# A windowed-attention and gated-MLP kernel: the first entry's values loaded behind its queries and keys, three of them by ScalarE's queue

## The chip, the cores and the metric

The kernel runs on one core of one Trainium2 chip. The metric is the device time of one launch in microseconds (us). TensorE, the matrix engine, is called PE; the others are VectorE (DVE), ScalarE (ACT), GpSimd (POOL) and SyncE (SP), which here only issues DMAs.

## The reference, cut to what matters

Attention over 8 batch entries, 8 heads, 576 positions and 64 dimensions per head, with a causal window; then the attention's output, 4,608 tokens of 512, goes through an MLP with a gate.

```python
scores = scale * np.matmul(q, k.transpose(0, 1, 3, 2))
mask_plain = (rel >= 0) & (rel < 32)                               # heads 0 to 3
mask_dil = (rel >= 0) & (rel < 128) & (rel % 4 == 0)               # heads 4 to 7
attn = softmax(np.where(masks, scores, -1e9))
x = np.matmul(attn, v)          # then (B*S, H*D)
h = x @ w_in                    # 512 x 2048
g = h * (1.0 / (1.0 + np.exp(-1.702 * h)))
out = g @ w_out                 # 2048 x 512
```

## The kernel before, in words

The MLP's products are made of three matmuls each: weights and inputs are split into a high part that PE's fast type can hold and a low part that is the rest, and high x high, low x high and high x low are summed. So every weight tile has to be decoded before its first use. `decode` (line 363) does it for one tile of 128 x 512: a DMA (`fetch`, line 392), two activations on ScalarE (lines 402 and 403), a third that may go to VectorE (line 396 or 398), a shift on VectorE (line 406), an addition on VectorE or GpSimd, a copy that rounds to the high part (line 346), and a subtraction that leaves the low part (line 353). The tiles are taken in the order of lines 360 and 361: the first two of the up-projection (n = 0 and 1), the first of the down-projection (n = 2), the third of the up-projection (n = 3), and so on.

Attention works on pairs of heads; one batch entry is four pairs, so pairs 0 to 3 are the first entry. For these `first_attention` (line 683) loads queries and keys with one DMA (`load_qk`, line 435), the values with another (`load_v`, line 448), makes the scores (line 478 puts the mask into the PSUM place `sp`, line 490 adds the products to it), and then the softmax: the maximum (line 510), the subtraction (in the helper of line 353), the exponentials on ScalarE (line 514), the sum (line 526), the reciprocal (line 518), the scaling by it (line 529). There is one `sp` place, so a pair's scores wait until the subtraction of the pair before has read it. `first_transposed` (line 691) turns the weights round and `first_multiplied` (line 697) multiplies them by the values (line 576) into the four PSUM banks `first_x`; `drain_x` (line 613) copies these into `xs`, again as a high and a low part, and the next pair's product waits for that. The products of PE's matrix with `xs` (line 863, tile `hp_m`) begin the MLP's first group of tokens.

Four loads of the first entry's values are the subject here. `load_v` puts those of pair 0 into a place of their own, `v`, and those of pairs 1 to 3 into parts of `arena` that later hold other things. Line 454 tells the planner of each load: a cost of 390 (KB) on the DMA resource, an urgency (lower goes first) and the earliest time at which it may be issued (0, 4, 11 and 14 us).

The order of all instructions on every engine is made by a planner before the launch (class `Plan`). Each step is added with its possible engines and their costs, an urgency, what it reads and writes, a slack (a gap that it must keep, for a step without predecessors the earliest time), and the count of PE instructions in it. `placed` (line 111) goes through simulated time: at each turn it takes the engine that can start something first, and of the steps that can start by then the one of lowest urgency. For a DMA the simulated data come over a bus (line 203). Where PE would be idle in the first 60 us of the plan it gets filler matmuls: small ones (line 1262, up to 25 us) and full ones (line 1258, tile `idle`), whose number is counted from the idle time expected. `ordered` (line 104) plans four times, from the second time on with latest starting times worked out from the plan before, which rule from 130 us on.

`fetched` (line 134) is the planner's model of the loading of PE's instructions: these come in blocks whose edges are at instruction 193 + 256 j; the block behind one edge is asked for when PE passes the edge before, and is there some time later: 4.2 us if that was before 6 us, 6.1 us before 18 us, 4.2 us after.

```python
                part = cost * (edge - n) / count
                at = max(when + part, blocks[j])
                blocks.append(at + (4.2 if at < 6.0 else 6.1 if at < 18.0 else 4.2))
```

All DMAs of the kernel before are issued by SP (`load = nc.sync.dma_start`, line 229), in the planner's order, one after the other, on one queue.

Of the kernel before, what the change touches and what calls it, by code (L numbers as in the profile page):

```python
# [15 lines left out]
B, H, S, D = 8, 8, 576, 64  # L16
DM, DF = 512, 2048
P = 128
NC = DM // P
# [14 lines left out]
QT = 5  # L34
# [8 lines left out]
PE, ACT, DVE, POOL, DMA = range(5)  # L43
# [4 lines left out]
class Plan:  # L48
# [9 lines left out]
    def add(self, costs, urgency, work, reads=(), writes=(), slack=0.0, count=0):  # L58

        i, after = len(self.ops), set()
        for k in reads:
            after.add(self.writer.get(k))
        for k in writes:  # L70
            after.add(self.writer.get(k))
            after.update(self.readers.get(k, ()))
        for k in writes:
            self.writer[k], self.readers[k] = i, []
        for k in reads:
            if k not in writes:
                self.readers.setdefault(k, []).append(i)
        self.ops.append((costs, (urgency, i), work, after - {None, i}, slack, count))
# [32 lines left out]
    def placed(self, warm_until, soon, late=None):  # L111
# [12 lines left out]
        issued, blocks = [0], [0.0]  # L124

        def start(i, e):
            held = port[0] if e == POOL or (e == DVE and ops[i][0][e] < 0) else 0.0
            if e == DMA and ops[i][1][0] >= 2000.0 and ops[i][0][e] > 100:
                held = bus[0] - 3.0
            if e == DMA and late is not None and SINCE < ready[i][e] < late[i] - CALM and late[i] < 9.0e3:  # L130
                held = max(held, ready[i][e] + 1.2)
            return max(free[e], ready[i][e], held)

        def fetched(count, when, cost):

            n = issued[0]
            issued[0] += count
            for j in range(len(blocks) - 1, 1 << 30):
                edge = 193 + 256 * j
                if edge >= n + count or edge > 1500:  # L140
                    return when + cost
                part = cost * (edge - n) / count
                at = max(when + part, blocks[j])
                blocks.append(at + (4.2 if at < 6.0 else 6.1 if at < 18.0 else 4.2))
                when, cost, n, count = at, cost - part, edge, count - (edge - n)

        open_ = [set() for _ in free]
# [5 lines left out]
        while any(open_):  # L153
# [6 lines left out]
            when, e = min((min(start(i, e) for i in mine[e]), e) for e in range(5) if mine[e])  # L160
# [22 lines left out]
            if e == PE and when < warm_until:  # L183

                at, size = max(free[e], 1.0), 0.26 if when > 8.0 else 0.44
                if when < SHORT and blocks[-1] < when - 0.3:

                    small = min((193 + 256 * (len(blocks) - 1) - issued[0]) // 4 + 1, int((when - at - 0.1) / 0.045))
                    order.extend([(None, e)] * small)
                    at = fetched(4 * small, at, small * 0.045)  # L190
                idle = max(0, int((when - max(at, 1.5) - 0.5) / size))
                fetched(2 * idle, at, idle * size)
                order.extend([(-1, e)] * idle)
            order.append((i, e))
            starts[i] = when
            if e == PE:
                cost = fetched(ops[i][5], when, cost) - when
# [19 lines left out]
def tile_windowed_attention_then_gated_mlp(  # L217
# [9 lines left out]
    nc = tc.nc  # L227
    V, A, G, T = nc.vector, nc.scalar, nc.gpsimd, nc.tensor
    load = nc.sync.dma_start
# [7 lines left out]
    add = plan.add  # L237
# [4 lines left out]
    def temp(shape, dt, tag, name):  # L242
        return tmp.tile(shape, dt, tag=tag, name=name)
# [175 lines left out]
    def lots(k):  # L419

        if 0 < k < NC:
            return f"first qk{k}", f"first v{k}"
        return "qk0", "v0"
# [15 lines left out]
    def load_v(k):  # L439
        u, place = pairs[k], lots(k)[1]  # L440

        def work(e):
            if k < NC:
                n = (QT if dilated(k) else QT + 1) * 2 * D
                flat = (None, late, main_x, left_x)[k][:, 2 * S:2 * S + n] if k else temp([P, n], F32, "v", f"v_{k}")
                u["v"] = flat.rearrange("p (s a d) -> p s a d", a=2, d=D)

                load(flat, first_v[k][:, 2 * D * (QT + 1) - n:])
                return
            flat = temp([P, 2 * NB * D], F32, "v", f"v_{k}")  # L450
            u["v"] = flat.rearrange("p (a s d) -> p a s d", a=2, s=NB)
            load(flat, vp[k - NC])

        add({DMA: 390 if k < NC else 328}, (-6.7, -6.7, -3.8, -1.6)[k] if k < NC else 1.6 * k - 0.3, work, waits(k),
            (place, place + "l"), (0.0, 4.0, 11.0, 14.0)[k] if k < NC else 0.0)

    def waits(k):

        return ["xh3.0"] if NC <= k < FIRST * NC else []

    def dilated(k):
        return k % NC >= NC // 2
# [220 lines left out]
    def first_attention(k):  # L683


        load_qk(k)
        load_v(k)
        add({PE: 1.5 if k else 2.3}, k - 1.0e5, lambda e: scores(k), (lots(k)[0],), ("sp", f"scores{k}"), count=180)
        softmax(k, k)
# [15 lines left out]
    def attention(k, urgency):  # L705
# [8 lines left out]
        if k == NC:  # L714
            load_qk(k)
            alone(k)
        load_v(k)
        if n and n > k + 1:
            if k == FIRST * NC:
# [481 lines left out]
    for i in range(4):  # L1201
# [6 lines left out]
    blocks = [Block("p", (3, 4), (dests[3], dests[4]), early_units, few=True),  # L1208
              Block("q", (5, 6), (dests[5], dests[6]), late_units),
              Block("r", (B, 7), (dests[B], dests[7]), late_units)]  # L1210
# [102 lines left out]
```

## Time and profile before

| | us |
|---|---|
| median of three timed runs | 823.56 |
| lowest and highest of them | 823.24, 824.2 |
| the profiled execution's own time | 822.45 |
| its span, from the first to the last instruction | 820.7 |
| TensorE busy in the span | 809.3 |
| VectorE, ScalarE, GpSimd busy | 669.0, 518.0, 328.4 |

A row of the timeline has the start in us from the span's start, the duration in us, the engine, the line of the kernel, the operation, what it writes and reads, and the number of like instructions that the row merges; in brackets stands the idle time of that engine before it and what ended it. PE rows are matmuls, PEld rows their weight loads, SPq rows issues of DMAs by SP. A row of the windows has the stretch, its length, then the busy time (and number of instructions) of PE, PEld, DVE, ACT and POOL, the granted clock of PE as a share, the busy share of the DMA engines and GB/s. In the list of DMA queues a row has the queue and its kind, then packets, MB and share of 16 engines' time.

### The profile page before, as it was taken

To read this page: it belongs to the slowest core of one execution; us is meant where nothing else is said; L and a number is where in the kernel's file an instruction comes from. 1 tells how busy PE (TensorE), PEld (TensorE's weight loads), DVE (VectorE), ACT (ScalarE), POOL (GpSimd) and SP (SyncE) were. 2 spreads that over 40 slices of the span, in tenths; PEclk is the share of its full clock that TensorE was granted. 3 is DMA by queue.
4 is the path that set the end of the run, shared out by engine and by line. 5 is a ranking of instruction groups with operands and counts; after the bars stand their busy time and mean duration, and the time that the engine had idled before them with its cause. 6 is when DMAs were issued, how large, how long until landed. Compare 5 with 4: busy or idle time off the path is not lost.

```text
span 820.7 us, 18890 instructions
## 1 busy us (share of the span) xinstructions
PE 809.3 (99%) x7279; PEld 653.4 (80%) x7279; DVE 669.0 (82%) x1081; ACT 518.0 (63%) x988; POOL 328.4 (40%) x294
## 2 busy tenths in 40 slices
PE   7999999999999999999999999999999999999997
PEld 4677878888887888778888888888888888888886
DVE  6898988888888876899889899996679885867575
ACT  7898986767577766786866654545456534544340
POOL 3442325455556553244345445531215332112251
PEclk9999999999999999999999999999999999999999
DMA  9577658899758657797788777775565658674545
GB/s 354 186 249 212 175 161 296 287 318 303 241 176 271 223 180 243 252 307 234 235 236 264 253 254 249 234 256 183 179 207 189 198 189 275 201 226 157 180 153 181
DMA packets 109610, 188.13 MB, mean 229 GB/s; under 512 B 26448, under 2 KB 55376, under 8 KB 109520
## 3 DMA queue, kind: packets, MB, share of 16 engines
q1 hardware_dynamic: 109376, 186.78, 70.2%
q8 instruction: 58, 0.95, 0.5%
q14 instruction: 32, 0.26, 0.1%
q10 hardware_dynamic: 144, 0.13, 0.0%
HBM read 140.64 MB, written 45.09 MB: 226 GB/s over the span
## 4 chain that ended last, share of the span: by engine, by line
PE 97%; DMA 1%; DVE 1%; issue 0%; ACT 0%; SPq 0%; DVEq 0%
PE hp_m L863 16%; PE up_p L1006 10%; PE up_r L1006 9%; PE up_q L1006 9%; PE acc_m L800 5%; PE second_p_Q L1121 5%; PE second_q_Q L1121 5%; PE acc_m L804 5%; PE acc_m L801 5%; PE second_r_Q L1121 5%; PE sp L490 4%; PE second_q_Z L1121 3%; PE second_r_Z L1121 3%; PE second_R L1121 3%; PE second_p_Z L1121 3%; PE av L608 2%
## 5 line engine op out<-in xcount | busy, mean ns | idle before, releaser
L353 POOL TENSOR_TENSOR arena<-arena 128x256 f32<-128x256 f32 (+3 forms) x94 | 100.7, 1083 | 97.8 <-DVE wi_last_units L353 21.6
L863 PE MATMUL hp_m<-xs,wi_kept 128*128 128x512 f32 x504 | 127.7, 396 | 1.2 <-DVE arena L872 0.9
L863 PEld LDWEIGHTS hp_m<-xs,wi_kept 128*128 128x128 f32 x504 | 92.9, 188 | 22.8 <-DVE arena L872 1.9
L353 POOL TENSOR_TENSOR wo_kept<-arena,wo_kept 128x512 fp32r<-128x512 f32 x41 | 56.9, 1395 | 131.5 <-ACT wo_kept L346 84.9
L346 ACT ACTIVATE wo_kept<-arena 128x512 fp32r<-128x512 f32 x111 | 69.2, 630 | 40.7 <-PE second_r_Q L1121 10.9
L1006 PE MATMUL up_r<-wi_kept,xs 128*128 128x512 f32 x336 | 85.3, 389 | 0.0
L1006 PE MATMUL up_p<-wi_kept,xs 128*128 128x512 f32 x336 | 84.2, 394 | 0.2 <-DVE arena L353 0.2
L1006 PE MATMUL up_q<-wi_kept,xs 128*128 128x512 f32 x336 | 83.4, 389 | 0.0
L1006 PEld LDWEIGHTS up_p<-wi_kept,xs 128*128 128x128 f32 x336 | 62.1, 188 | 14.7 <-DVE arena L353 0.9
L1006 PEld LDWEIGHTS up_q<-wi_kept,xs 128*128 128x128 f32 x336 | 63.0, 188 | 13.3 <-DVE arena L1028 0.3
L1006 PEld LDWEIGHTS up_r<-wi_kept,xs 128*128 128x128 f32 x336 | 63.1, 188 | 13.1
L353 DVE TENSOR_TENSOR wo_kept<-arena,wo_kept 128x512 fp32r<-128x512 f32 x80 | 61.1, 775 | 5.1 <-ACT wo_kept L346 4.7
L346 ACT ACTIVATE bt<-ct 32x256 f32<-32x256 f32 (+1 forms) x130 | 56.6, 435 | 11.7 <-DVE ct L534 6.0
L353 POOL TENSOR_TENSOR pr<-pr,sm 128x320 f32<-128x320 f32 x52 | 43.7, 856 | 48.5 <-DVE sm L518 43.5
L800 PE MATMUL acc_m<-gh,wo_kept 128*128 128x512 f32 x156 | 61.5, 394 | 0.0
L353 POOL TENSOR_TENSOR wo_kept<-wi_last_units,wo_kept 128x512 fp32r<-128x512 f32 x22 | 29.9, 1361 | 78.3 <-ACT wo_kept L346 72.3
L353 DVE TENSOR_TENSOR arena<-arena 128x512 f32<-128x512 f32 (+1 forms) x75 | 59.1, 797 | 2.7 <-ACT arena L346 1.8
L801 PE MATMUL acc_m<-gh,wo_kept 128*128 128x512 f32 x156 | 60.8, 390 | 0.0
L1027 ACT ACTIVATE arena<-arena 128x512 f32<-128x512 f32 x60 | 37.4, 628 | 33.4 <-DVE arena L353 27.2
L1028 DVE SCALAR_TENSOR_TENSOR arena<-arena 128x512 f32<-128x512 f32 x60 | 49.8, 837 | 1.7 <-ACT arena L1027 1.3
L346 ACT ACTIVATE gh<-arena 128x512 fp32r<-128x512 f32 x57 | 36.0, 631 | 17.5 <-DVE arena L872 5.8
L353 DVE TENSOR_TENSOR gl<-arena,gh 128x512 fp32r<-128x512 f32 x53 | 41.3, 779 | 6.5 <-ACT gh L346 3.2
(267 smaller groups left out, 1824.7 us busy)
## 6 DMA issues: line engine op xcount, KB each, us to landing
xs<-sums SPq DMA_DIRECT2D x168, 256.0 KB, 3.3
out_weights<-sums_o SPq DMA_DIRECT2D x63, 512.0 KB, 3.5
qk<-qk_dram SPq DMA_DIRECT2D x29, 576.0 KB, 4.4
xs<-sums_o SPq DMA_DIRECT2D x21, 512.0 KB, 3.8
v<-vp_dram SPq DMA_DIRECT2D x28, 320.0 KB, 4.1
sums_o<-arena SPq DMA_DIRECT2D x32, 256.0 KB, 3.2
sums<-arena SPq DMA_DIRECT2D x32, 256.0 KB, 2.9
arena<-wi_dram SPq DMA_DIRECT2D x15, 512.0 KB, 4.7
```

What stands on the lines that cost most here:

```text
L346: A.activation(dst, src, AF.Copy, scale=scale)
L353: (V if e == DVE else G).tensor_tensor(out=dst, in0=a, in1=b, op=op)
L490: T.matmul(dst[:, w:w + n], u["qk"][rows, at:at + 32], u["qk"][rows, S + first:S + first + n], start=not masked(k), stop=True, tile_positi ...
L608: T.matmul(u["x"][i][rows, at:at + last - first], u["v"][keys, a, m], bt[keys, m, a, first:last], start=(bank_, a) not in begun, stop=True ...
L800: T.matmul(self.acc[j], w[:, 0, cols], high, start=f == 0, stop=False)
L801: T.matmul(self.acc[j], w[:, 1, cols], high, start=False, stop=False)
L804: T.matmul(self.acc[j], w[:, 0, P * j:P * j + P], low, start=False, stop=f == NF - 1)
L863: T.matmul(hps[f], wi(f)[:, st, cols], mv[:, c], start=c == 0 and k == 0, stop=c == NC - 1 and k == 2)
L1006: T.matmul(self.banks[place], xs[:, slot, at:at + P], wi_kept[:, 2 * a + c, mv], start=fresh and c == 0 and k == 0, stop=c == 1 and k == 2 ...
L1027: add({ACT: 0.60}, -10.0, lambda e: A.activation(unit(tmp), src(), AF.Tanh, scale=0.851), need, own(tmp))
L1028: add({DVE: -0.70 if need[0][0] == "A" else 0.70}, -10.0, lambda e: V.scalar_tensor_tensor(out=unit(dst), in0=unit(tmp), scalar=1.0, in1=s ...
L1121: T.matmul(self.second[key], w[:, st, cols], mv, start=fresh and y == 0 and k == 0, stop=y == 1 and k == 2, skip_group_check=True)
```

## The change

Three things change in the code.

In `load_v`, the values of pair 0 get the urgency -2.4 instead of -6.7. So SP issues them behind the queries and keys of pairs 1 and 2 (-5.7, -4.7) and the weight tiles n = 1, 2 and 3 (-5.7, -4.6, -2.5), and just ahead of the queries and keys of pair 3 (-2.3).

The values of pairs 1 to 3 become a step of ScalarE, with a cost of 0.06 us in the plan, the urgency -50 (ahead of all else that can start) and the earliest times 16, 18 and 20 us; their DMAs are issued by `nc.scalar.dma_start`, so in ScalarE's order of instructions and on its queue. In the plan they no longer take time on the bus.

In `fetched`, the time of 6.1 us holds for edges passed before 12 us, not 18 us.

```diff
-                blocks.append(at + (4.2 if at < 6.0 else 6.1 if at < 18.0 else 4.2))
+                blocks.append(at + (4.2 if at < 6.0 else 6.1 if at < 12.0 else 4.2))
...
-                load(flat, first_v[k][:, 2 * D * (QT + 1) - n:])
+                (nc.scalar.dma_start if e == ACT else load)(flat, first_v[k][:, 2 * D * (QT + 1) - n:])
...
-        add({DMA: 390 if k < NC else 328}, (-6.7, -6.7, -3.8, -1.6)[k] if k < NC else 1.6 * k - 0.3, work, waits(k),
-            (place, place + "l"), (0.0, 4.0, 11.0, 14.0)[k] if k < NC else 0.0)
+        add({ACT: 0.06} if 0 < k < NC else {DMA: 390 if k < NC else 328}, (-2.4, -50.0, -50.0, -50.0)[k] if k < NC else 1.6 * k - 0.3,
+            work, waits(k), (place, place + "l"), (0.0, 16.0, 18.0, 20.0)[k] if k < NC else 0.0)
```

Since the plan is made from all steps at once, the order on every engine can come out differently, also far behind the opening.

## The prediction

> **What bounds the kernel now.** I read the page first, then the windows by stage, the timeline of the first 40 us and the waits.
>
> ```profile
> span 820.7 us, 18890 instructions
> PE 809.3 (99%) x7279; PEld 653.4 (80%) x7279; DVE 669.0 (82%) x1081; ACT 518.0 (63%) x988; POOL 328.4 (40%) x294
> PE 97%; DMA 1%; DVE 1%; issue 0%; ACT 0%; SPq 0%; DVEq 0%
> ...
> 0.00:40.00 40.00, 34.59 (x896) 22.77 (x897) 29.43 (x65) 33.44 (x52) 17.29 (x25) 0.96 0.72 266
> 40.00:130.00 90.00, 89.05 (x1020) 70.63 (x1019) 80.91 (x142) 79.19 (x139) 30.09 (x27) 1.00 0.67 205
> 130.00:300.00 170.00, 169.91 (x2174) 138.40 (x2174) 142.43 (x248) 122.10 (x267) 94.81 (x102) 1.00 0.78 258
> ```
>
> TensorE is the bound. The first two columns of a window are its length and PE's busy time: from 40 us on PE loses 0.95 us in 90 and then 0.09 in 170. Only in the first 40 us is there something to win: 5.41 us idle, and filler matmuls (line 1258) that count as busy. The change can act there alone, through the instant from which PE is fed without a break; every microsecond by which that instant moves moves the end by as much.
>
> The opening stage, row by row:
>
> ```profile
> 1.71 0.44 SPq L448 DMA_DIRECT2D v<-first_v_dram  x1
> 2.19 0.43 SPq L435 DMA_DIRECT2D arena<-qk_dram  x1
> 5.96 0.38 SPq L448 DMA_DIRECT2D arena<-first_v_dram  x1
> 7.22 1.34 ACT L396 ACTIVATE arena<-arena 128x512 f16<-128x512 f32 x1
> 8.71 0.74 ACT L514 ACTIVATE pr<-pr 128x640 f32<-128x640 f32 x1 [0.15 <-DVE pr L353]
> 8.74 0.71 PE L478 MATMUL sp<-plain,ident 128*128 128x320 bf16 x2 [0.65 <-DVE pr L353]
> 9.38 1.34 PEld L490 LDWEIGHTS sp<-arena 64*32 64x32 f32 x84 [0.52 <-DMA arena<-qk_dram]
> 10.58 0.67 ACT L402 ACTIVATE arena<-arena 128x512 f32<-128x512 f32 x1 [0.61 <-DMA arena<-wi_dram]
> 10.76 2.74 PE L1258 MATMUL idle<-ident 128*128 128x512 bf16 x6
> 11.73 0.82 DVE L353 TENSOR_TENSOR pr<-sp,mx 128x640 f32<-128x640 f32 x1
> 13.29 0.74 PE L478 MATMUL sp<-arena,ident 128*128 128x320 bf16 x2
> 15.03 2.33 PE L1258 MATMUL idle<-ident 128*128 128x512 bf16 x10
> 17.56 0.86 PE L490 MATMUL sp<-arena 64*32 64x64 f32 x65
> 20.25 0.37 PE L490 MATMUL sp<-arena 64*32 64x64 f32 x19 [1.83 <-issue]
> 20.55 1.49 PE L576 MATMUL first_x<-ct,v 32*64 32x32 f32 x92
> 21.96 2.63 PE L1258 MATMUL idle<-ident 128*128 128x512 bf16 x6
> 22.90 0.76 DVE L353 TENSOR_TENSOR xs<-first_x,xs 128x432 fp32r<-128x432 f32 x2
> 24.53 1.16 PE L576 MATMUL first_x<-ct,arena 32*64 32x32 f32 x92
> ```
>
> The scores of pairs 0 to 3 (line 490) follow each other through one PSUM place, each waiting for the softmax of the one before; then come the products with the values (line 576), each waiting for the drain of the one before. Pair 0's values are read first at 20.55, pair 1's at 24.53. Between them stand a hole of 1.83 us in the middle of pair 3's scores (20.25), and six fillers that took 2.63 us although the drain they cover ends at about 22.90 + 0.76 = 23.66: some 0.85 us too long.
>
> The hole is "issue": no semaphore explains it. It is the loading of PE's instructions:
>
> ```profile
> 0.00:14.38 14.38, 11.02 (x354) 6.67 (x355) 8.74 (x26) 10.06 (x15) 4.12 (x12) 1.00 0.87 332
> 0.00:20.24 20.24, 15.06 (x479) 9.08 (x479) 13.20 (x34) 15.59 (x22) 7.63 (x17) 1.00 0.91 354
> 0.00:24.60 24.60, 19.41 (x604) 11.53 (x607) 16.96 (x41) 18.88 (x30) 9.40 (x18) 0.93 0.90 345
> q8 instruction: 7, 0.11, 1.0%
> ```
>
> The PE and PEld counts give 709 instructions up to 14.38, 958 up to 20.24 and 1,211 up to 24.60, and the kernel's model (line 139) puts block edges at 705, 961 and 1,217. The seven packets of that queue up to 45 us make 16 KB each. So a block asked for at 14.38, when an edge was crossed, was there at 20.25: 5.87 us. The one asked for at 20.25 was needed at 24.60, where no such hole shows: at most 4.35 us. The Trainium skill (Runtime: NRT & Kernel Launch, Instruction fetch mechanics) has blocks of 256 instructions and calls their fetch mostly hidden: the size agrees, the 1.83 us does not.
>
> **The change, part by part.** One: pair 0's values go from third to eighth place in SP's queue. They are needed at 20.55 and five transfers later they land still far ahead of it: nothing lost. What stood behind them comes earlier:
>
> ```profile
> 5.00:10.00 5.00, 4.35 (x171) 2.73 (x175) 3.11 (x6) 4.07 (x6) 0.00 (x1) 1.00 0.99 378
> 15.00:20.00 5.00, 3.42 (x86) 1.79 (x77) 3.84 (x9) 4.67 (x7) 3.27 (x4) 1.00 1.02 408
> v<-first_v_dram SPq DMA_DIRECT2D x1, 384.0 KB, 6.2
> ```
>
> 384 KB at 378 GB/s are 1.04 us. Pair 1's queries then land near 8.3, and its wait of 0.52 us goes; the masks of the same scores start at 8.74 behind pair 0's subtraction and last 0.71 anyway, so I count 0.3. The second weight tile lands near 9.55 instead of 10.58.
>
> Two: that earlier landing changes the planner's order. With its own costs (line 203: 360 KB per us after 2 us, and 0.2 us of latency; they set an order, no time here is taken from them) the second weight tile is ready for ScalarE at 8.39 and pair 0's exponentials at 8.51. So its first activation (line 402) is now put ahead of the exponentials (line 514), where it stood behind them. In rows:
>
> ```profile
> 9.48 0.83 DVE L526 TENSOR_REDUCE sm<-pr 128x10 f32<-128x650 f32 x1 [0.20 <-ACT pr L514]
> 10.87 0.82 DVE L510 TENSOR_REDUCE mx<-sp 128x10 f32<-128x640 f32 x1 [0.56 <-PE sp L490]
> 11.61 0.20 DVE L518 RECIPROCAL sm<-sm 128x10 f32<-128x10 f32 x1
> 11.98 1.97 SPq L448 DMA_DIRECT2D arena<-first_v_dram  x2
> 12.47 0.43 DVE L406 TENSOR_SCALAR arena<-arena 128x512 uint32<-128x512 uint32 x1
> 18.65 0.67 ACT L402 ACTIVATE arena<-cell 128x512 f32<-128x512 f32 x1 [0.34 <-DMA cell<-wo_dram]
> 31.46 0.68 DVE L353 TENSOR_TENSOR wi_kept<-arena,wi_kept 128x512 fp32r<-128x512 f32 x1
> ```
>
> On the chip ScalarE is free at 7.22 + 1.34 = 8.56 and must wait for the landing near 9.55; with 0.67 for that activation the exponentials start near 10.25 instead of 8.71. VectorE then works in a row from 10.25: the second tile's shift 0.43, the first tile's low part 0.68, pair 0's sum 0.83, pair 1's maximum 0.82, the reciprocal 0.20, pair 1's subtraction 0.82. That ends near 14.05 instead of 11.73 + 0.82 = 12.55. Pair 2's scores waited behind six fillers to 13.29; they now start near 14.15: 0.85 later.
>
> Three: pairs 1 to 3's values leave SP's queue for ScalarE's, not before 16, 18 and 20 us of the plan. They are read at 24.53 and later. SP's issue of such a load lasted 0.38 (5.96); on ScalarE, 93% busy in 15:20 (4.67 of 5), three cost between nothing, if the activation before is still running, and 3 x 0.44 = 1.32, if the queue stands. No row shows one on ScalarE. The nearest row, SP's 0.38, is of an engine with no other work; on ScalarE the activation issued just before still runs for up to 1.34 (7.22), so I take 0.1 on the path. Behind a standing issue would queue the exponentials of pair 2 and the drain copies, and for these wait VectorE and PE. The Trainium skill (DMA: Bandwidth & Descriptors, Issuing engines are not separate DMA queues) says that loads of either engine share the same 16 DMA engines, so only issuing time is saved; no run here shows a second queue yet. In SP's queue the next weights move up, for which ScalarE waited 0.34 (18.65); with PE in the hole at that time, I count it at nothing.
>
> Four: the block model expects 4.2 us instead of 6.1 for edges crossed at 12 to 18 us. That only alters the count of fillers and the order, but the real fetch decides. Its edge is crossed some 0.85 us later, near 15.2. The fetch time lies between 4.35 and 5.87. For the upper end speaks that the DMA engines stay full (1.02, 408 GB/s); for the lower that the two loads issued from 11.98 on no longer stand in the queue when it is asked for. Neither row is nearer; I take 5.0. The block is there near 20.2; what is left of pair 3's scores then takes 0.5, and pair 0's product starts near 20.7 (20.55 before): +0.15. The hole shrinks from 1.83 to some 0.4 us, so the six fillers behind the product fall between 6 x 0.23 (the pitch at 15.03) and 6 x 0.44 (at 21.96), say 2.0 instead of 2.63: pair 1's product near 24.2, -0.3 against 24.53. With 0.1 for ScalarE's issues the feeding of PE starts 0.2 us earlier.
>
> From 40 us on the same matmuls follow. The whole order is planned anew, so holes can come or go: the largest one there is 0.95 (the 40:130 row), and I allow that much either way.
>
> **The sum.** The profiled execution took 822.45 (span 820.7): less 0.2 it is 822.25. The three timed runs lie 1.11 higher in the median (823.56), so 823.4. What a measurement here can tell from no change is about 0.2%, 1.65 us: from 821.9 to 825.2.
>
> **The rivals.** *Faster: the hole closes.* If the fetch takes 4.35 or less and the exponentials do not fall behind, nothing holds pair 3's scores: 1.83 go, PE keeps its clock and the fillers' 0.85 go too: 2.7 in all, 820.9. For it: the hole is the largest single loss, and the softmax chain alone had pair 3 begun by 17.56. Against it: DMA stays full, and part two delays the chain by itself. The rule quoted above from the Trainium skill (Runtime: NRT & Kernel Launch, Instruction fetch mechanics), a fetch mostly hidden, would make it so. Chance 0.22.
>
> *Slower: ScalarE's order.* The exponentials wait for a transfer they do not need. If the 1.55 us by which they are late (10.25 against 8.71) pass through all four pairs and the block, asked for later, takes its 5.87 again, the hole no longer swallows the delay; the three issues add up to 1.32, say 0.5: 2.0 in all, 825.6. It decides if pair 3's scores end after 22.1 instead of 20.62. For it: ScalarE works strictly in order and has no slack in 15:20. Against: the fillers and the hole give 0.7 and 1.83 of cover. Chance 0.17.
>
> *Nothing arrives at PE.* The values were never waited for, and if the block lands at 20.25 as before, all else is cover: 823.6. Chance 0.06; the forecast has 0.55.
>
> **How the numbers follow.** The forecast's own range is 822.2 to 824.6: 0.8 either way for the fetch time (4.35 to 5.87), the rest for ScalarE's issues. The range of 8 in 10 reaches into both rivals, to 821.1 and 825.3. Faster by over 0.2% has the first rival and a little of the forecast's edge, 0.25; slower the second and as little, 0.19; the rest, 0.56, is no difference.
>
> **What would show it.** Right: line 402 before the first line 514 on ScalarE, that exponential near 10.2; pair 2's masks near 14.2; an "issue" hole of under 1 us in pair 3's scores; pair 0's product at 20.4 to 21.0 and pair 1's at 23.9 to 24.6; ScalarE's three issues between 16 and 21 us with no wait of PE on a load of values; PE full from 40 us on but for about 1 us. Wrong: no issue hole and pair 1's product before 23 (the first rival), pair 3's scores ending past 22 (the second), a product that waits for its values, or new idle time of PE over 1 us after 40 us, which would show that the order of the rest decided.

## The result, and the profile after

| | before | after |
|---|---|---|
| median of the timed runs, us | 823.4 (4 runs) | 834.93 (4 runs) |
| lowest and highest | 823.08, 824.2 | 834.05, 835.8 |
| profiled execution, us | 822.45 | 835.33 |

The ratio is 1.014, with an interval of 1.0125 to 1.0155: 11.5 us slower, where the prediction allowed 1.9. The page of the changed kernel, its totals and the engines' shares of the chain that ended last:

```profile
span 833.6 us, 19007 instructions
PE 811.2 (97%) x7335; PEld 654.4 (78%) x7335; DVE 661.0 (79%) x1075; ACT 519.3 (62%) x999; POOL 320.2 (38%) x289
...
PE 86%; DMA 6%; DVE 4%; ACT 2%; issue 1%; SPq 0%; POOL 0%; DVEq 0%; ACTq 0%
```

The span grew by 12.9 us. PE's busy time grew by 1.9 (811.2 against 809.3); the other 11.0 is PE standing idle. Where it stands is read from the windows, whose first columns are stretch, length, and PE's busy time:

```profile
0.00:40.00 40.00, 30.08 (x931) 19.99 (x932) 27.00 (x59) 29.20 (x43) 13.78 (x22) 0.87 0.61 229
40.00:130.00 90.00, 88.21 (x948) 69.85 (x947) 79.04 (x138) 80.22 (x143) 29.77 (x25) 1.00 0.65 205
130.00:300.00 170.00, 167.93 (x2230) 135.80 (x2229) 143.87 (x247) 120.06 (x266) 98.35 (x104) 1.00 0.80 261
300.00:500.00 200.00, 197.08 (x1791) 158.84 (x1791) 164.22 (x268) 135.77 (x290) 76.87 (x67) 1.00 0.76 241
```

The row of before that the prediction does not show is

```profile
300.00:500.00 200.00, 199.82 (x1805) 161.59 (x1804) 175.09 (x277) 135.92 (x283) 89.86 (x72) 1.00 0.78 253
```

Length less busy time gives 9.92, 1.79, 2.07 and 2.92 us of idle time; before it was 5.41, 0.95, 0.09 and 0.18. So the loss has two places: the opening, and stages more than 100 us behind the loads that the change moves. The opening, in PE's rows of the timeline:

```profile
11.39 3.73 PE L1258 MATMUL idle<-ident 128*128 128x512 bf16 x11
14.96 0.43 PE L478 MATMUL sp<-arena,ident 128*128 128x320 bf16 x2
15.32 1.07 PE L490 MATMUL sp<-arena 64*32 64x64 f32 x84
16.33 0.71 PE L1262 MATMUL idle<-ones 32*32 32x16 f32 x62
19.49 0.45 PE L478 MATMUL sp<-arena,ident 128*128 128x320 bf16 x2 [2.45 <-DVE pr L353]
19.86 0.32 PE L490 MATMUL sp<-arena 64*32 64x64 f32 x8
21.62 1.38 PE L490 MATMUL sp<-arena 64*32 64x64 f32 x76 [1.44 <-issue]
22.93 1.18 PE L576 MATMUL first_x<-ct,v 32*64 32x32 f32 x52
25.07 0.93 PE L576 MATMUL first_x<-ct,v 32*64 32x64 f32 x40 [0.96 <-issue]
25.93 3.59 PE L1258 MATMUL idle<-ident 128*128 128x512 bf16 x8
29.46 1.61 PE L576 MATMUL first_x<-ct,arena 32*64 32x32 f32 x92
...
45.82 0.50 PE L800 MATMUL acc_m<-gh,wo_kept 128*128 128x512 f32 x1 [1.79 <-ACT gh L346]
```

Against the rows of before, pair 2's masks start at 14.96 (13.29), pair 3's at 19.49 (17.20), pair 0's product at 22.93 (20.55), pair 1's at 29.46 (24.53), and the first matmul of the down-projection (line 800) at 45.82. Of that last one the row of before is

```profile
39.63 0.39 PE L800 MATMUL acc_m<-gh,wo_kept 128*128 128x512 f32 x1
```

so PE is 6.2 us behind there, and has done three matmuls of line 863 less by then (36 against 39). At equal work, the 200th matmul that writes `hp_m` or `acc_m`, it is 7.0 us behind (89.60 against 82.60). No product waits for its values. What differs is the order: eleven full fillers where six stood, 62 small filler matmuls (31 steps) where ten full ones stood, and a second hole marked "issue". Behind the opening, three of the new holes:

```profile
150.78 1.55 PE L863 MATMUL hp_m<-xs,wi_kept 128*128 128x512 f32 x6 [1.31 <-issue]
...
345.80 3.02 PE L1006 MATMUL up_p<-wi_kept,xs 128*128 128x512 f32 x12 [0.93 <-DMA xs<-sums]
...
394.15 1.19 PE L1121 MATMUL second_p_R<-wo_kept,out_weights 128*128 128x512 f32 x4 [1.61 <-DMA out_weights<-sums_o]
```

What released the first is a block of PE's instructions (its 16 KB moved from 148.40 to 149.37), and the other two ended with loads that the first entry's values have nothing to do with.

### The profile page after: what moved, and what is told of

It reads as the page before. It is cut to its first block, busy times and chain, and to the rows that moved or that the text cites. A ratio compares the mean times of both kernels' runs of the same rounds, so it can differ in the third digit from the quotient of the medians.

```text
span 833.6 us, 19007 instructions
## 1 busy us (share of the span) xinstructions
PE 811.2 (97%) x7335; PEld 654.4 (78%) x7335; DVE 661.0 (79%) x1075; ACT 519.3 (62%) x999; POOL 320.2 (38%) x289
## 4 chain that ended last, share of the span: by engine, by line
PE 86%; DMA 6%; DVE 4%; ACT 2%; issue 1%; SPq 0%; POOL 0%; DVEq 0%; ACTq 0%
PE hp_m L863 13%; PE up_p L1006 9%; PE up_r L1006 8%; PE up_q L1006 8%; PE second_q_Q L1121 5%; PE second_p_Q L1121 5%; PE second_r_Q L1121 5%; PE acc_m L800 5%; PE acc_m L801 5%; PE acc_m L804 4%; DMA out_weights<-sums_o 4%; PE sp L490 3%; PE second_r_Z L1121 3%; PE second_q_Z L1121 3%; PE second_R L1121 3%; PE second_p_Z L1121 3%
## 5 line engine op out<-in xcount | busy, mean ns | idle before, releaser
L353 POOL TENSOR_TENSOR arena<-arena 128x256 f32<-128x256 f32 (+3 forms) x100 | 107.5, 1081 | 126.8 <-DVE wo_kept L353 27.5
L346 ACT ACTIVATE wo_kept<-arena 128x512 fp32r<-128x512 f32 x116 | 72.6, 629 | 46.4 <-PE second_r_Q L1121 10.4
L353 POOL TENSOR_TENSOR wo_kept<-arena,wo_kept 128x512 fp32r<-128x512 f32 x33 | 44.7, 1358 | 110.5 <-ACT wo_kept L346 71.7
L353 DVE TENSOR_TENSOR wo_kept<-arena,wo_kept 128x512 fp32r<-128x512 f32 x88 | 67.6, 776 | 7.0 <-ACT wo_kept L346 6.6
L353 POOL TENSOR_TENSOR wo_kept<-wi_last_units,wo_kept 128x512 fp32r<-128x512 f32 x24 | 32.9, 1373 | 98.8 <-ACT wo_kept L346 90.2
L353 DVE TENSOR_TENSOR arena<-arena 128x512 f32<-128x512 f32 (+1 forms) x71 | 52.2, 739 | 1.5 <-ACT arena L346 1.0
L1028 DVE SCALAR_TENSOR_TENSOR arena<-arena 128x512 f32<-128x512 f32 x60 | 46.3, 781 | 0.7 <-ACT arena L1027 0.2
```

What stands on the lines that cost most here:

```text
L346: A.activation(dst, src, AF.Copy, scale=scale)
L353: (V if e == DVE else G).tensor_tensor(out=dst, in0=a, in1=b, op=op)
L1028: add({DVE: -0.70 if need[0][0] == "A" else 0.70}, -10.0, lambda e: V.scalar_tensor_tensor(out=unit(dst), in0=unit(tmp), scalar=1.0, in1=s ...
```

## The experiments

Two theories stood at the start. *Loads*: the values on ScalarE's queue, or pair 0's behind five transfers, delay something. *Order*: the loads cost nothing, and the time goes to the order in which the planner now puts all other steps. "Order" here takes in the engine that the planner chooses for a step and the fillers that it sets. In the expectations of the first four runs, theory A is one way in which the order could do it (the early second weight tile), B is the loads, and C is the block model with its 12 us. The changes are shown against the kernel before or the changed kernel, as said; every ratio is to runs of the kernel before that were taken beside it (medians 823.3 to 823.7).

**One part of the change alone.** The kernel before with the one edit, and last the changed kernel with 18 put back.

```diff
const12:  else 6.1 if at < 12.0 else 4.2   (was 18.0)
v0late:   (-2.4, -6.7, -3.8, -1.6)[k]      (first was -6.7)
actonly:  pairs 1 to 3 on ScalarE, -50.0, earliest 16, 18, 20; pair 0 as before
after18:  the whole change, but at < 18.0
```

> The kernel before with the 12 instead of the 18 in the block model alone; all loads as before. Theory A (order: the change is slow because the earlier second weight tile puts its decoding ahead of the first exponentials and the planner's order comes out worse from there on): line 402 stays behind line 514, so 822 to 826. Theory B (the loads themselves: ScalarE's issues, or values that come late): 822 to 826 as well. Theory C (the block model: fillers are counted for a block that comes later than planned): 829 or more.

> The kernel before with pair 0's values at urgency -2.4 alone; 18 in the model, the other values on SP as before. Theory A: the second weight tile comes early here too, so line 402 goes ahead of line 514 and most of the loss is there: 829 or more. Theory B: nothing is issued by ScalarE and no values come late, so 822 to 826. Theory C: 822 to 826.

> The kernel before with only the values of pairs 1 to 3 moved to ScalarE (16, 18, 20 us); pair 0's values third as before, 18 in the model. Theory A: line 402 stays behind line 514, so at most the order of the rest shifts: 822 to 827. Theory B: ScalarE's issues cost here as in the change: 829 or more. Theory C: 822 to 826.

> The whole change but with 18 left in the block model. Theory A: as slow as the change or slower, 830 or more, since the second tile still comes early. Theory B: the same, 830 or more. Theory C: back to 822 to 826.

| | median, us | ratio and interval | pair 0's product | first of line 800 |
|---|---|---|---|---|
| const12 | 834.01 | 1.014 (1.0121 to 1.0159) | 21.60 | 42.40 |
| v0late | 830.93 | 1.0099 (1.0083 to 1.0116) | 22.33 | 43.90 |
| actonly | 831.33 | 1.0112 (1.009 to 1.0135) | 21.00 | 40.47 |
| after18 | 830.34 | 1.0083 (1.0062 to 1.0103) | 22.86 | 45.28 |

Each part alone costs 7.6 to 10.7 us, the two moves of loads together 7.0 (after18), so they don't add up. The 12.0 alone, which moves none of the four loads and adds no step to the kernel's own, costs 10.7, nearly as much as the whole change. It does change fillers and engines: VectorE gets 1,086 instructions in place of 1,081, GpSimd 285 in place of 294. None of the three theories as written holds: const12 came out as only C had it, v0late as only A, actonly as only B, and after18 as A and B had it. What all four share is a new order, which speaks for *Order* at large.

The places differ too. At the 200th matmul that writes `hp_m` or `acc_m` the four are 2.6, 4.7, 1.6 and 5.6 us behind the kernel before (85.20, 87.26, 84.23 and 88.15 against 82.60), so const12 and actonly lose most of their time behind the opening.

**Loads and order apart.** The first kernel has the order of before for every step and only the values' loads in their new places; the second has the order of the changed kernel, with the loads back on SP's queue in their old places.

```diff
# old_order_new_loads: before, in ordered()
+        order = [x for x in order if x[0] not in values]
+        order.insert(at + 1, (values[0], DMA))          # behind the fourth weight tile
+            order.insert(at, (i, ACT))                  # pairs 1 to 3: at 16, 18, 20 us
# new_order_old_loads: after, in ordered()
+        order = [x for x in order if x[0] not in values]
+        behind = dict(zip(values, (1, 7, 10, 10)))
+            order.insert(fetches[behind[i]] + 1, (i, DMA))
```

> The order of all other instructions is that of the kernel before, fillers too; only the four loads of values stand where the change wants them: pair 0's on SP behind the fourth weight tile, the others issued by ScalarE ahead of its first steps planned at 16, 18 and 20 us. Theory A (the order is what costs, not the loads): 822 to 825. Theory B (the loads cost: ScalarE's issues, late values): 827 or more.

> The order of all other instructions is that of the changed kernel, fillers too; the four loads of values are put back to their old places on SP's queue (third, behind pair 3's queries, two behind the next weights). Theory A: as slow as the change or slower, 833 to 838. Theory B: most of the loss goes, 828 or less.

The new loads in the old order gave 823.25 (0.9997, 0.9986 to 1.0009); the old loads in the new order 835.25 (1.0153, 1.0136 to 1.017). That settles it: the loads cost nothing measurable, the order all of it. Nor does it cost anything that the program is another one, as long as the order stays. The timeline of the first:

```profile
5.37 1.44 PE L498 MATMUL sp<-qk 64*32 64x64 f32 x84 [0.40 <-DMA qk<-qk_dram]
...
20.20 0.37 PE L498 MATMUL sp<-arena 64*32 64x64 f32 x19 [1.25 <-issue]
20.50 1.16 PE L584 MATMUL first_x<-ct,v 32*64 32x32 f32 x92
...
39.60 0.39 PE L808 MATMUL acc_m<-gh,wo_kept 128*128 128x512 f32 x1
```

Its helper text moves the line numbers by 8. It starts 0.48 us later than before (5.37 against 4.89) and reaches line 800's matmul at 39.60 against 39.63: the hole of 1.83 shrank to 1.25 and took the delay in.

**Which stretch of the order.** One kernel takes the new plan for the steps that it starts before 70 us and the order of before for the rest, one the reverse; cut22 is the first with the cut at 22 us. All have the new loads, but old_opening has the old ones.

```diff
+CUT = 70.0
+        done = {i for i, o in enumerate(ops) if starts[i] < CUT}
+        order = [(i, e) for i, e in order[:last + 1] if i in done or i is None or i < 0]
+        order += [(i, e) for i, e in other if i is not None and i >= 0 and i not in done]
```

> Both plans are made; the steps that the changed plan starts before 70 us run in its order with its loads, all later ones in the order of the plan before. In the changed profile the first down-projection matmul starts at 45.8 us against 39.6. Theory A1 (the opening alone is to blame): 834 or more. A2 (the opening costs its 6 us and the order of the rest costs the others): 828 to 831. Theory B: 834 or more, since the loads are here as in the change.

> Both plans are made; the steps that the old plan starts before 70 us run in its order with its loads, all later ones in the order of the changed plan. Theory A1 (the opening alone): 822 to 825. A2 (the rest of the order costs some 5 us by holes behind 130 us): 827 to 830. Theory B: 822 to 825.

> The new plan's order for the steps that it starts before 22 us, so the scores of the first entry and what the other engines do beside them, and all else in the order before, with the new loads. The new order up to 70 us cost 8.8. If most of that lies in the scores and in what precedes them (the fillers and VectorE's order there), this gives 829 to 832; if it lies in the drains and in the first products of the MLP behind them, 824 to 826.

New opening: 832.27 (1.0115, 1.01 to 1.013), +8.8. Old opening: 826.13 (1.0042, 1.0027 to 1.0057), +2.6. Together 11.4, so opening and rest make up the whole. Neither theory's range held: the first time lies between A1's 834 and A2's 831, the second between A1's 825 and A2's 827. The division is not sharp, since a seam between two plans can make holes of its own. In the profile of new_opening a wait of 0.91 us stands at 78.93, where neither the changed kernel nor the one before has one, and the changed kernel's own profile puts 7.0 us of its loss before the 200th of those matmuls and the other 5.9 behind. Read it as 7 to 9 us for the opening and 3 to 6 for the rest.

The cut at 22 us gave 830.26 (1.0079, 1.0066 to 1.0093), +6.7. That would put most of the opening's loss into the order of the first entry's scores, but it is not shown: the old order behind the cut got holes of its own, and this kernel reaches the first matmul of the down-projection at 47.52, later even than new_opening (46.50):

```profile
25.22 0.93 PE L590 MATMUL first_x<-ct,v 32*64 32x64 f32 x40 [1.23 <-issue]
27.88 1.58 PE L590 MATMUL first_x<-ct,arena 32*64 32x32 f32 x87 [1.72 <-ACT pr L528]
32.25 0.40 PE L590 MATMUL first_x<-ct,arena 32*64 32x16 f32 x5 [2.80 <-issue]
```

**ScalarE's swap.** The kernel with the old order and the new loads, and line 402 of the second tile ahead of pair 0's exponentials: the step to which the prediction gave most of its slower rival.

```diff
+        order.remove((shift, ACT))
+        order.insert(order.index((exponentials, ACT)), (shift, ACT))
```

> The old order with the loads moved (823.25 against 823.5), and one thing more: on ScalarE the second weight tile's first activation goes ahead of pair 0's exponentials, as in the change; nothing else moves. Theory A-swap (this exchange is what makes the new opening slow): pair 2's scores start 0.8 later or more and the end comes 4 or more later, 827 to 832. Theory A-fillers (the fillers and the block edges that the new plan counts make it slow): the hole and the fillers swallow most of it, 823 to 825.5.

823.45 (1.0002, 0.9993 to 1.0011). In the old order the swap costs nothing measurable: the fillers and the hole in pair 3's scores cover it. Inside the new order it was not tried alone.

**The fillers.** The changed kernel without the small fillers behind pair 2's scores (no_small), and also with three full fillers in place of eight behind pair 0's product (no_small_few, run again as few_again).

```diff
+        order[third:fourth] = [x for x in order[third:fourth] if x[0] is not None]
+        for n in reversed(fillers[3:]):      # no_small_few alone
+            del order[n]
```

> The changed kernel without the 31 small fillers (124 PE instructions) that its plan sets between the scores of pairs 2 and 3. Theory A-fillers: the block that ends the hole then stands further behind in pair 3's scores, and pair 0's product has no second hole of 0.96: 2 us off, 832 to 833.5. Theory A-swap: as the change, 834.5 to 836.

> The changed kernel without the 31 small fillers (832.12) and with three instead of eight full fillers between the first two products. In the run before they ended at 27.1, the drain that they cover at 26.1. Theory A-fillers: pair 1's product moves up by about 1 us and so does the end, 830.5 to 831.5. Theory A-vector (VectorE's own chain sets the opening, fillers or not): 831.7 to 832.5.

> The changed kernel without the small fillers and with three full ones, a second time, as the base of the next run: 831.2 if the first time was right, whose interval was wide.

Without the small ones 832.12 (1.0111, 1.0096 to 1.0126): 2.8 less than the changed kernel, with intervals that just touch. They push the block edge forward in the program, so that 8 of pair 3's 84 scores run ahead of it (65 before). With fewer full ones as well 831.22 (1.01, 1.0069 to 1.013) and 830.05 (1.0088, 1.007 to 1.0106); the interval of each takes in the other, and the gain over no_small, 0.9 to 2.1, is hardly beyond them. In the profile of few_again, which is of its slowest execution (833.47), PE waits in their place:

```profile
19.80 0.72 PE L484 MATMUL sp<-arena,ident 128*128 128x320 bf16 x2 [4.01 <-DVE pr L359]
20.44 1.45 PE L496 MATMUL sp<-arena 64*32 64x64 f32 x84
...
26.07 1.74 PE L582 MATMUL first_x<-ct,arena 32*64 32x32 f32 x92 [1.95 <-ACT arena L352]
```

**VectorE's order.** In the changed kernel the rounding copy of the second weight tile (line 348) and its low part stand between two steps of pair 2's softmax chain; before, ScalarE made that copy (line 346, 14.79):

```profile
12.82 0.82 DVE L353 TENSOR_TENSOR pr<-sp,mx 128x640 f32<-128x640 f32 x1
14.24 0.93 DVE L348 CAST wi_kept<-arena 128x512 fp32r<-128x512 f32 x1 [0.59 <-POOL arena L353]
15.20 1.09 DVE L353 TENSOR_TENSOR wi_kept<-arena,wi_kept 128x512 fp32r<-128x512 f32 x1
16.21 0.82 DVE L526 TENSOR_REDUCE sm<-pr 128x10 f32<-128x650 f32 x1
16.95 0.81 DVE L510 TENSOR_REDUCE mx<-sp 128x10 f32<-128x640 f32 x1
17.68 0.89 DVE L695 STREAM_TRANSPOSE ct<-pr 128x320 f32<-128x320 f32 x2
18.50 0.17 DVE L518 RECIPROCAL sm<-sm 128x10 f32<-128x10 f32 x1
18.61 0.83 DVE L353 TENSOR_TENSOR pr<-sp,mx 128x640 f32<-128x640 f32 x1
```

The next kernel is no_small_few with these two steps behind pair 2's subtraction. Its second weight tile's parts are made from words that a later tile has already overwritten, so only its time is read.

```diff
+        order = [x for x in order if x[0] not in late_parts]
+        order[at + 1:at + 1] = [(i, DVE) for i in late_parts]
```

> The same, and VectorE's two steps for the second weight tile (its copy and its low part, 14.4 to 16.5 us in the trace) moved behind pair 2's subtraction; nothing else. Theory A-vector: they stand in the way of pair 2's maximum and subtraction, so pair 3's scores start 1 to 1.5 earlier and the end comes 1 or more earlier than without this step. Theory A-fillers: no difference, within 0.5 us.

832.88 (1.0105, 1.0079 to 1.0131): no gain that shows, though these intervals are too wide to tell a gain of 1 us. Pair 3's masks moved from 19.83 to 18.82, and the block of instructions took it back:

```profile
18.82 0.45 PE L490 MATMUL sp<-arena,ident 128*128 128x320 bf16 x2 [2.59 <-DVE pr L365]
19.19 0.95 PE L502 MATMUL sp<-arena 64*32 64x64 f32 x70
21.46 0.48 PE L502 MATMUL sp<-arena 64*32 64x48 f32 x14 [1.31 <-issue]
```

**The drain.** no_small_few again, with VectorE's last part of pair 1's drain named behind ScalarE's copies in the program; each engine's own order stays.

```diff
+        order.insert(first[-1], order.pop(lows[0]))
```

> As the run before it, but the text of the program names VectorE's subtraction of a drain behind ScalarE's copies of that drain; each engine's own order is the same. If ScalarE's wait of 0.67 and VectorE's of 0.42 in that drain are made by the order in which the program names them, and reach PE, 1 us less than the run before it; if they are covered, no difference.

832.16 (1.0101, 1.0085 to 1.0117), no faster than few_again, which was measured beside it. The two waits are gone, but the third pair's product starts at 30.32 against 30.27: they were covered.

**New orders that have nothing to do with the change.** The kernel before with one of the planner's own numbers moved by a hair; loads and instructions are those of before. In two of them the order is the same as before, step for step, to 57 us (exp076) or 170 us (bus361); in gate061 each engine's own order is the same to 57 us.

```diff
bus361:   cost / 361.0          (was 360.0, line 203)
exp076:   add({ACT: 0.76}, ...  (was 0.75, line 514)
gate061:  add({ACT: 0.61}, ...  (was 0.60, line 871)
```

> The kernel before with one number of the planner changed that has no bearing on the chip: the simulated bus has 361 instead of 360 KB per us. Order and loads are as before up to 170 us; from there on about a third of PE's steps and three quarters of the vector engines' come in another order. Theory D (the old order is a good one among many, and any new planning costs some us): 825 to 830. Theory E (a new order costs only where the change disturbs the opening): 822.5 to 824.5.

> The kernel before with the planner's cost of the exponentials at 0.76 us instead of 0.75. The order is as before up to 57 us and another one from there on. Theory D: 825 to 832. Theory E: 822.5 to 824.5.

> The kernel before with the planner's cost of the gate's tanh at 0.61 instead of 0.60 us. The order is as before up to 57 us and another one from there on; the plan's own end is 816.1 us against 817.4 of the kernel before, 819.4 of the change and 817.9 of exp076. If the plan's own length tells which order is better: 821 to 823. Theory D (any new planning costs some us): 825 to 830.

826.62 (1.004, 1.0026 to 1.0055), 827.71 (1.0048, 1.0028 to 1.0068) and 827.9 (1.0054, 1.0034 to 1.0073): 3.3 to 4.4 us slower each. Not all of this is shown to be the order's. In bus361's profile the block in pair 3's scores came late (a hole of 2.94), and it is already 1.8 us behind at the masks that start at 72.97 in before (74.77), where its order is still that of before; its profiled execution is 4.5 us longer than before's (826.96 against 822.45). exp076 reached line 800's matmul at 39.83, 0.2 behind, and lost its time further on, in small holes and in matmuls (PE busy for 810.9 us against 809.3):

```profile
40.00:130.00 90.00, 90.00 (x1017) 71.51 (x1019) 83.97 (x145) 76.14 (x133) 34.35 (x27) 1.00 0.67 213
130.00:300.00 170.00, 168.78 (x2198) 136.38 (x2180) 139.73 (x241) 121.98 (x271) 93.29 (x103) 1.00 0.75 248
300.00:500.00 200.00, 198.62 (x1799) 160.22 (x1798) 171.99 (x276) 135.94 (x291) 75.30 (x64) 1.00 0.79 256
```

Idle there: none, 1.22 and 1.38, against 0.95, 0.09 and 0.18. None of eight newly planned orders (these three, the five kernels of the whole change or a part of it) came out within 0.2% of the one before. By the planner's own simulated time gate061 is the shortest of all (816.12 against 817.36 for before); on the chip it is 4.2 us slower.

## Why the prediction was wrong

The step that failed is the allowance for the new order: "The whole order is planned anew, so holes can come or go: the largest one there is 0.95 (the 40:130 row), and I allow that much either way." The order alone costs 11.7 us (new_order_old_loads, 835.25 against 823.5); cut at 70 us it is 8.8 with the opening and 2.6 behind it, a division that the seam blurs. The size was taken from the holes that the old order has, and these say nothing about another order. Even the 0.95 entered neither the sum nor the range, whose width was given to the fetch time and ScalarE's issues. A kernel that stands idle for 1.27 us between 40 and 700 us can lose much and win hardly anything by a new order; that much the windows of before did show. With it went the allowance's place: the prediction kept before's fillers, engines and block edge in the opening and let them only start later.

By its own steps:

One, the loads, was right, and so was the first half of two:

```profile
9.58 0.67 ACT L402 ACTIVATE arena<-arena 128x512 f32<-128x512 f32 x1 [0.39 <-DMA arena<-wi_dram]
10.15 0.73 ACT L514 ACTIVATE pr<-pr 128x640 f32<-128x640 f32 x1
```

Nothing waits for the values, the second weight tile was there at 9.58 (predicted 9.55), and old_order_new_loads prices all of it at 0.9997. Line 402 stands ahead of the exponentials, which start at 10.15 (predicted 10.25), and swap_only shows that this costs nothing in the old order. But pair 2's masks started at 14.96, not 14.15: VectorE was done with pair 1's subtraction at 12.82 + 0.82 = 13.64, ahead of the 14.05 worked out, and eleven fillers, not six, held PE to 15 us. Their number was part of the plan that was being replaced. Pair 0's product then came at 22.93 (20.7 worked out), pair 1's at 29.46 (24.2).

Three was right in its price; the first issue came earlier than the 16 us forecast. The issues on ScalarE lasted 0.37, 0.34 and 0.33:

```profile
13.87 0.37 ACTq L448 DMA_DIRECT2D arena<-first_v_dram  x1
...
17.55 0.34 ACTq L448 DMA_DIRECT2D arena<-first_v_dram  x1
...
19.53 0.74 ACT L514 ACTIVATE pr<-pr 128x640 f32<-128x640 f32 x1
19.64 0.33 ACTq L448 DMA_DIRECT2D arena<-first_v_dram  x1
```

and the last of them, for one, lay beside a running activation. By the Trainium skill (DMA: Bandwidth & Descriptors, Issuing engines are not separate DMA queues) loads of either engine run on the same 16 DMA engines, and only issuing time is saved. The ratio of 0.9997 agrees with that; the sharing itself no run here shows.

Four took the fetch at 5.0 within 4.35 to 5.87. The first block came outside that. The windows count 702, 958 and 1,214 instructions of PE and PEld at three instants, with block edges at 705, 961 and 1,217:

```profile
0.00:15.51 15.51, 11.46 (x347) 6.88 (x355) 9.33 (x26) 10.94 (x16) 3.85 (x12) 1.00 0.89 343
0.00:21.60 21.60, 13.68 (x479) 8.55 (x479) 14.98 (x35) 15.96 (x23) 5.49 (x14) 0.98 0.93 357
0.00:25.06 25.06, 16.17 (x607) 10.82 (x607) 17.00 (x39) 17.52 (x24) 6.42 (x16) 0.91 0.84 322
```

The block came 6.1 us behind its edge, at 21.62 instead of 20.2, and the next 3.45 us behind that one. Both holes are real, but the larger error is that the step gave the shorter assumption (12 in place of 18 us) no price: "That only alters the count of fillers and the order". const12 shows 10.7 us for it alone.

The slower rival had the sign and the mark ("pair 3's scores ending past 22"; they ended at 21.62 + 1.38 = 23.0) but not the cause: its mechanism is the swap, which is worth nothing in the old order. The last mark in the list, idle time of PE over 1 us after 40 us "which would show that the order of the rest decided", is what came, beside the opening.

Still open is how the opening's part divides. The small fillers are some 2.8 of it. Taking out full fillers, VectorE's two steps or the drain's waits gave some 2 us at most, and in the profiles a wait or a hole stood in the place of what was taken out. Which step of the later order makes each hole behind 130 us was not tried. Nor was PE's clock, which was granted at half for longer than before. The first row is of the changed kernel, the second of the kernel before:

```profile
20.65:30.89 10.24, 8.31 (x268) 5.56 (x268) 7.58 (x15) 5.80 (x10) 5.07 (x6) 0.50 0.35 116
20.95:24.36 3.41, 3.41 (x78) 1.71 (x65) 3.29 (x7) 2.34 (x7) 1.06 (x1) 0.50 0.80 282
```

PE worked 8.31 us at half clock against 3.41. The 4.90 more would have taken half as long at full clock, so an estimate of what the clock took is 2.4 us, less what fell on fillers (3.59 of the 8.31) that only cover a wait.

## What to carry to other kernels

Where an order is planned from all steps at once, an edit is two changes: what it does, and a new order for everything else. Price the second by measuring orders that differ for no reason (a cost moved by 0.01), and split the two by keeping the old order and moving only what was meant. If PE is busy all but about 1 us behind the opening, a new order has next to nothing to win and, here, 3 to 12 us to lose.

## What the runs showed of the hardware beyond that

A block of PE's instructions came 3.45 us (after, 21.62 to 25.07), 5.4 us (old_order_new_loads, 14.82 to 20.20), 6.1 us (after, 15.51 to 21.62) and 7.0 us (bus361, 14.55 to 21.57, and cut22, 25.22 to 32.25) behind the crossing of its edge. The traces divide this time. In each of the five, one packet of 16 KB on the instruction queue (q8) took 0.9 to 1.1 us, and PE went on 1.5 to 1.6 us after its end. What differs is when the packet starts: 1.0, 2.8, 3.6, 4.4 and 4.5 us behind the crossing, in the order given. In cut22, the last, the DMA engines moved nothing from 25.2 to 27 us, so full DMA engines alone do not explain the late start; PE itself waited for ScalarE from 26.15 to 27.88 there. What sets the start was not tried. The Trainium skill (Runtime: NRT & Kernel Launch, Instruction fetch mechanics) calls the fetch mostly hidden; holes of up to 2.94 us in these runs say that it isn't in this opening. Behind 40 us the changed kernel's profile has one such hole of over 0.6 us (1.31, at 150.78), which agrees.

The clock granted to PE fell to 0.5 in the opening of most of these kernels, in stretches of 3.41 us or a multiple of it: 3.41 in before (20.95 to 24.36), 10.24 in after (20.65 to 30.89), 17.07 in cut22 (20.58 to 37.65). Fillers show it: the eight at 25.93 took 3.59 us, 0.45 each; ten of before's at 15.03 took 2.33, 0.23 each. In these three the stretch is longer where PE stood idle longer between 12 and 40 us (2.05, 5.87 and 10.22 us), but old_opening, idle for 3.40, has none; what sets it was not tried.

The first load landed up to 0.6 us apart in kernels whose first loads are the same: PE's first scores started at 4.89 (before), 5.38 (const12) and 5.51 (drain_fix). With the old order that did not reach the end: old_order_new_loads started them at 5.37 and its profiled execution took 822.22, before's 822.45.
